# An attention and gated-FFN kernel: one group of heads of the second query block moved up to second place, more V tiles before the loop, later splitting of the exponentials, and finer background pieces

## The chip, the cores and the metric

The kernel runs on one core of a Trainium2 chip. The metric is the device time of one execution in microseconds; lower is better. The profile is of one execution.

## The reference

The input x has 2048 rows of 512 numbers. The layer normalises x, runs attention with 32 heads of 16 numbers, adds the result to x, normalises again, runs a gated feed-forward part with 1792 hidden columns, and adds that too.

```python
    h = x + _A_ref(_layernorm(x, axis=-1), A_wqkv, A_wo)
    h2 = h + _B_ref(_layernorm(h, axis=-1), B_w_gate, B_w_up, B_w_down)
...
        scores = jnp.einsum("bhqd,bhkd->bhqk", q, k) * (Dh ** -0.5)
        p = _softmax(scores, axis=-1)
        o = jnp.einsum("bhqk,bhkd->bhqd", p, v)
...
        h = _sigmoid(g) * u
        return jnp.einsum("bsf,fd->bsd", h, w_down)
```

## The kernel before, in words

**Units and groups.** The queries are cut into 4 blocks `qc` of 512, the heads into 8 groups `g` of 4, the keys into 16 tiles `kt` of 128. One unit is (qc, g, kt, j): 128 keys by 512 queries of head j of the group. The 2048 units stand in one list, block by block and group by group, 64 units to a group, and are taken three at a time as 683 tiles. A tile's scores go to three PSUM banks `pss` (two such buffers, L679); ScalarE takes their exponential into `pt` (five buffers, L828); TensorE multiplies `pt` with the V tile into the single accumulator `acc` (L747). When all 64 units of a group are in, `finish_group` transposes `acc` into `xs` on VectorE (L721), divides by the row sums, and after every second group turns the result into `OT`. Only then may the next group write `acc`.

**Splitting.** For some tiles the third unit's exponential is made on VectorE instead (`dexp_first`: one read of the scores, L761, and six more steps to `dr`, L781), and ScalarE takes two banks rather than three. `split` allows it only where the tile's last unit has `kt < NT - 4`, where no long VectorE work is pending, and where fewer than three such units are open.

**Background work.** Projections of K, Q and V, the output projection with the second normalisation (`wo_ln`), and the feed-forward part (`ffn`) are generators in one queue `bg`; its head advances when tokens and readiness allow, two matmuls at a time, through one PSUM bank `pm`. The order of all instructions is written by a planner in the kernel which keeps its own clocks `T["P"]`, `T["A"]` and `T["D"]` for TensorE, ScalarE and VectorE. `force(tag)` empties the queue down to a tag that the next scores or V products need. `prep_q` for block qc + 1 is inserted at position 1 of the queue, behind the item at its head, each time a pair of groups ends; `ffn(qc)` is one item. Q and K reach their place (`QT`, `KT`) by DMAs on SyncE's queue (`spread`, L172, then the row `sh`, L485); the shift row needs a maximum over K that also makes a trip by DMA (`k<-kr`, L451, then `kcol`, L454).

**When V products are issued.** Within the planner's time for one tile, `av` runs if six or more finished units are ready, or three or more after background work had its turn. A remainder of one or two at the end of a group waits until it is five tiles old (`NPT`) and is then forced.

**Before the loop.** A prologue normalises x, transposes it, makes K and Q of group 0 straight into place (`k0`, `proj0`) and the first six V tiles (`NV0`). The other V tiles, K and Q are background work, in the order V 6 to 9, K and Q of group 1, V 10 to 15, then K and Q of the other pairs. **After the loop** a tail does the last block's output projection and feed-forward part.

Of the kernel before, what the change touches and what calls it, by code (L numbers as in the profile page):

```python
# [10 lines left out]
BF16 = mybir.dt.bfloat16  # L11
# [3 lines left out]
ALU = mybir.AluOpType  # L15
# [13 lines left out]
def kernel(  # L29
# [47 lines left out]
    xnT = [const.tile([P, DC, QC], BF16, name=f"xnT{c}") for c in range(NQC)]  # L77
    KT = [const.tile([P, S], BF16, name=f"KT{g}") for g in range(NG)]
    QT = [const.tile([P, QC], BF16, name=f"QT{g}") for g in range(NG)]
    Vaug = const.tile([P, NT, H, VW], BF16)  # L80
    wq_sb = const.tile([P, DC, D], BF16)
    wo_sb = const.tile([P, NP, D], BF16)
    kcol = [const.tile([8, 1], FP32, name=f"kcol{p}") for p in range(NP)]
    o2buf = [const.tile([P, QC // 32, 32], BF16, name=f"o2_{i}") for i in range(2)]

    pre = ExitStack()
    prep = pre.enter_context(tc.tile_pool(name="prep", bufs=1))
# [91 lines left out]
    def v_out(ps, t, act):  # L179
        dst = Vaug[:, t, :, 0:DH]  # L180
        src = ps.rearrange("p (h d) -> p h d", d=DH)
        if act:
            nc.scalar.copy(out=dst, in_=src)
        else:
            nc.vector.tensor_copy(out=dst, in_=src)
# [6 lines left out]

    nc.scalar.activation(out=small.tile([P, 1], FP32, name="warm")[:], in_=eps_t[:], func=ACT.Sqrt)

    NV0 = 6
    mvs = [small.tile([P, TQ, nc.vector.BN_AGGR_DIM], FP32, name="mv") for c in range(NQC)]
    rstds = [small.tile([P, TQ], FP32, name="rstd") for c in range(NQC)]
    kmin = small.tile([P, NQC], FP32, name="kmin", bufs=1)
# [3 lines left out]
    def s0(c, *tiles):  # L202
        for i in tiles:
            ln_stats(xb[c][:, i, :], mvs[c][:, i, :])
# [43 lines left out]
    def kred0(c, pm):  # L248
        nc.vector.tensor_reduce(out=kmin[:, c:c + 1], in_=pm, axis=AX.X, op=ALU.min)

    def v0(t, act=True):
        ps = bank0()
        v_mm(ps, t)
        v_out(ps, t, act)

    s0(0, 0, 1, 2)
    act_stats(xb[0][:, 3, :], mvs[0][:, 3, :])
# [18 lines left out]
    s0(2, 1, 2, 3)  # L276
    rs0(2)
    pq, sqq = proj0(0, 1)
    nc.tensor.matmul(pq, lhsT=selq[:], rhs=sqq[:], start=False, stop=True, skip_group_check=True)
    pk1 = k0(1)  # L280
    s0(3, 0)
    a0(2)
    for i in range(TQ):
        t0(2, i)
    v0(0)
    s0(3, 1, 2, 3)
    rs0(3)
    pk2 = k0(2)
    v0(1)
    kred0(0, pk0)  # L290
    a0(3)
    for i in range(TQ):
        t0(3, i, i % 2 == 1)
    kred0(1, pk1)
    kred0(2, pk2)
    pk3 = k0(3, True)
    nc.scalar.activation(out=small.tile([P, 1], FP32, name="warm")[:], in_=eps_t[:], func=ACT.Exp)
    kred0(3, pk3)
    nc.vector.tensor_reduce(out=kfull[:], in_=kmin[:], axis=AX.X, op=ALU.min)
    nc.vector.tensor_scalar(out=QT[0][:], in0=pq, scalar1=kfull[:, 0:1], scalar2=None, op0=ALU.add)  # L300
    for t in range(2, NV0):
        v0(t, t % 2 == 0)
    for g in range(1, NG):
        ones_fill(g)
    ps0ctx.close()
# [7 lines left out]
    def pm_tile():  # L313
        return ps_m.tile([P, 512], FP32, name="pm")[:]
# [146 lines left out]
    def prep_q(qc, p, groups=(0, 1)):  # L461
# [131 lines left out]
        nc.scalar.activation(out=th[:], in_=ps, func=ACT.Tanh, scale=0.5)  # L593
        return th

    def ffn(qc):
        hT = fpool.tile([P, FC, QC], BF16, name="hT")
        th = {}
        for f in range(FC):
            yield pe(2, pm_new())  # L600
            ps = pm_tile()
            gate_mm(ps, wg, f, 0, 2)
            yield pe(2)
            gate_mm(ps, wg, f, 2, 4)
            ja = st["pm"] = act(530, lambda ps=ps, f=f: th.update({f: tanh_out(ps)}), st["mark"])
            yield pe(2, pm_new())
            ps = pm_tile()
            gate_mm(ps, wu, f, 0, 2)
            yield pe(2)
            gate_mm(ps, wu, f, 2, 4)  # L610
            st["pm"] = dve(700, lambda ps=ps, f=f: glu_out(hT, f, th[f], ps), st["mark"], ja)
        for i in range(TQ):
            ps = None
            for f in range(0, FC, 2):
                if (qc, i, f) == (NQC - 2, TQ - 1, 0):
                    yield pe(2, pm_new(), HOLD)
                else:
                    yield pe(2, pm_new() if f == 0 else None)
                if f == 0:
                    ps = pm_tile()  # L620
                down_mm(ps, hT, i, f, f + 2)
            st["pm"] = dve(700, lambda ps=ps, i=i: down_out(ps, qc, i), st["mark"])
        yield pe(0, st["pm"])

    HOLD = Mark(None)
    bg = deque()
    done = {("q", 0, 0)} | {("v", t) for t in range(NV0)}

    def queue(gen, tag, at=None):
        bg.insert(len(bg) if at is None else min(at, len(bg)), [gen, tag, None])  # L630
# [30 lines left out]
    def force(tag):  # L661
        while tag not in done:
            flush()
            try_bg(1e9, 1e12)

    units = [(qc, g, kt, j) for qc in range(NQC) for g in range(NG)
             for kt in range(NT) for j in range(4)]
    tiles = [units[i:i + GU] for i in range(0, len(units), GU)]

    readers = {}  # L670
# [1 line left out]

    def scores(n):
        for qc, g, kt, j in tiles[n]:
            if (qc, g) != (0, 0):
                force(("q", qc, g // 2) if (qc, g) != (0, 1) else ("q", 0, 0, 1))
        pss = ps_s.tile([P, GU, QC], FP32, name="pss")
        for ui, (qc, g, kt, j) in enumerate(tiles[n]):
            mm = nc.tensor.matmul(pss[:, ui, :],  # L679
                                  lhsT=KT[g][32 * j:32 * j + 32, kt * P:(kt + 1) * P],  # L680
                                  rhs=QT[g][32 * j:32 * j + 32, :],
                                  start=True, stop=True, tile_position=(32 * j, 0))
            for r in readers.get(n - 2, ()) if ui == 0 else ():
                tc.add_manual_dep(mm.ins, r.ins.name,
                                  DependencyInfo(DependencyClass.Sync, DependencyReason.DATA),
                                  reason="both readers of the bank's last scores")
        T["P"] = max(T["P"], ex_end.get(n - 2, 0.0) + LAT) + 380
        sc_end[n] = T["P"]
        return pss
# [9 lines left out]
    def finish_group(qc, g):  # L699
        xs = work.tile([P, QC // 32, 32], FP32, name="xs")  # L700
        p, a = divmod(g, 2)
        o2 = o2buf[p % 2]

        def norm():
            rec = small.tile([P, QC // 32, 1], FP32, name="rec")
            nc.vector.reciprocal(out=rec[:], in_=xs[:, :, DH:VW])
            nc.vector.tensor_tensor(out=o2[:, :, DH * a:DH * a + DH], in0=xs[:, :, 0:DH],
                                    in1=rec[:].to_broadcast([P, QC // 32, DH]), op=ALU.mult)

        def turn():  # L710
            ot = otp.tile([P, QC], BF16, name="ot")
            nc.vector.transpose(out=ot[:], in_=o2[:].rearrange("p b r -> p (b r)"))
            OT[qc, p] = ot
            if qc + 1 < NQC:
                queue(prep_q(qc + 1, p), ("q", qc + 1, p), 1)
                if p == NP - 2:
                    XR.extend(load_xr(qc, i) for i in range(2))
            if g == NG - 1 and qc < NQC - 1:
                queue(wo_ln(qc), ("wo", qc))
                queue(ffn(qc), ("f", qc))  # L720
        j = st["acc"] = dve(730, lambda: nc.vector.transpose(  # L721
            out=xs[:].rearrange("p b r -> p (b r)"), in_=acc[:]), Mark(T["P"]))
        j = dve(680, norm, j)
        if a:
            otj[qc, p] = dve(720, turn, j)

    def av_ready(loose):
        return [un for un in avq if un.u[0] * NG + un.u[1] == st["cur"] and un.end is not None
                and un.end + LAT <= T["P"] + loose]

    def av(limit, loose=60.0):
# [61 lines left out]
        nc.sync.dma_start(out=wd_[:], in_=B_w_down.rearrange("(f p) n -> p f n", p=P))  # L793
        return wg_, wu_, wd_

    for t in range(NV0, NV0 + 4):
        queue(prep_v(t), ("v", t))
    queue(prep_k(0, (1,)), ("k", 0))
    queue(prep_q(0, 0, (1,)), ("q", 0, 0, 1))
    for t in range(NV0 + 4, NT):  # L800
        queue(prep_v(t), ("v", t))
    for p in range(1, NP):
        queue(prep_k(p), ("k", p))
        queue(prep_q(0, p), ("q", 0, p))
# [7 lines left out]
    for n, tl in enumerate(tiles):  # L812
# [4 lines left out]
        while any(un.n <= n - NPT for un in avq):  # L817
            flush()
            if not av(8, 1e12):
                break  # L820
        start = max(T["A"], sc_end[n] + LAT)
        pend = sum(c[0] for c in chain)
        split = (len(tl) == GU and tl[-1][2] < NT - 4 and pend <= 900 and len(live_d) < 3
                 and max(T["D"], sc_end[n] + LAT) + pend <= start + 900
                 and sum(j.ns for j in dq if j.ready() is not None) <= 1500)
        wa = len(tl) - split
# [18 lines left out]
        while T["P"] < lim - 150:  # L845
            run_dve(min(T["P"], hor))
            ready = len(av_ready(60.0))
            if ready >= 6 and av(8):
                continue
            used = try_bg(tokens)  # L850
            if used:
                tokens -= used
                continue
            if ready >= 3 and av(8):
                continue
            T["P"] += 100
        run_dve(hor)
# [121 lines left out]
```

## Time and profile before

| what | value |
|---|---|
| median of 4 runs | 1079.19 us (1078.11 to 1080.51) |
| the profiled execution | 1078.11 us, its span 1076.3 us |
| busy TensorE, VectorE, ScalarE | 834.7, 750.6, 904.9 us |
| granted clock of TensorE, mean | 0.833 |

The span runs from the first to the last instruction. Busy time is the union of an engine's instructions, so instructions of one engine that overlap are counted once. An idle time is put down to the engine whose work ended it.

### The profile page before, as it was taken

The page shows a single profiled execution, that of the slowest core. Times are in us where ns is not written, and L with a number is a line of the kernel's source. Part 1 is how long each engine was busy: PE and PEld are TensorE (multiplying, and loading weights), DVE is VectorE, ACT ScalarE, POOL GpSimd, SP SyncE. Part 2 cuts the span into 40 slices and gives each one's busy share as a digit, 9 for nine tenths or more (in the row PEclk, how much of TensorE's full clock was granted, in tenths as well). Part 3 has the DMA queues.
Part 4 walks back from the last instruction along what each step waited for, and adds up shares of the span by engine and source line. Part 5 has one row for each costly group of instructions (what it writes and reads, how often), then busy time and mean ns, then how long its engine had stood idle before and what let it go on. Part 6 is the DMA issues. An engine that isn't in the chain of part 4 may idle for free.

```text
span 1076.3 us, 14506 instructions
## 1 busy us (share of the span) xinstructions
PE 834.7 (78%) x5137; PEld 231.4 (22%) x5213; DVE 750.6 (70%) x1854; ACT 904.9 (84%) x799; POOL 2.9 (0%) x7
## 2 busy tenths in 40 slices
PE   4858678677778788788687877877688787786868
PEld 2211122112112222222121222212122221221223
DVE  8936555777668887877877877766587777776441
ACT  6826699899889999999988999989799898998632
POOL 1000000000000000000000000000000000000000
PEclk9965788657568999989876998989877898896689
DMA  8010111600000000000000000000100000000000
GB/s 279 1 32 1 25 27 30 211 10 6 1 2 15 1 1 2 1 20 11 16 16 1 1 1 2 1 15 11 31 25 1 1 1 1 1 11 5 1 5 20
DMA packets 22048, 22.63 MB, mean 21 GB/s; under 512 B 4828, under 2 KB 20504, under 8 KB 21976
## 3 DMA queue, kind: packets, MB, share of 16 engines
q1 hardware_dynamic: 20344, 20.59, 6.6%
q10 hardware_dynamic: 1632, 1.11, 0.3%
q8 instruction: 41, 0.67, 0.3%
q14 instruction: 31, 0.25, 0.1%
HBM read 11.93 MB, written 2.10 MB: 13 GB/s over the span
## 4 chain that ended last, share of the span: by engine, by line
ACT 32%; PE 26%; DVE 20%; issue 16%; SPq 4%; DMA 2%; ACTq 0%; DVEq 0%
ACT pt L828 28%; PE pss L679 8%; PE acc L747 6%; DVE J L761 4%; DVE dr L781 3%; SPq L172 3%; PE pm L573 2%; PE pm L165 2%; ACT th L593 2%; DVE dq L779 2%; DVE db L777 2%; DVE da L770 1%; PE pm L176 1%; PE gu L573 1%; PE hp L944 1%
## 5 line engine op out<-in xcount | busy, mean ns | idle before, releaser
L828 ACT ACTIVATE pt<-pss 128x1536 bf16<-128x1536 f32 (+1 forms) x683 | 855.0, 1406 | 111.5 <-PE pss L679 74.4
L679 PE MATMUL pss<-QT,KT 32*128 32x512 bf16 x2048 | 309.6, 444 | 159.0 <-ACT pt L828 120.3
L747 PE MATMUL acc<-pt,Vaug 128*17 128x512 bf16 x1851 | 300.6, 454 | 8.2 <-DVE xs L721 7.3
L761 DVE TENSOR_SCALAR J<-pss 128x512 uint16<-128x512 f32 x197 | 134.8, 684 | 120.5 <-PE pss L679 119.7
L679 PEld LDWEIGHTS <-KT 32*128 32x128 bf16 x2048 | 89.8, 93 | 440.3 <-issue 333.7
L781 DVE SCALAR_TENSOR_TENSOR dr<-J,dq 128x512 uint16<-128x512 uint16 x197 | 135.4, 687 | 4.5
L747 PEld LDWEIGHTS <-Vaug 128*17 128x17 bf16 x2048 | 56.8, 89 | 194.8 <-issue 190.7
L747 PE MATMUL acc<-dr,Vaug 128*17 128x512 bf16 x197 | 84.4, 443 | 8.3 <-DVE xs L721 6.5
L779 DVE TENSOR_TENSOR dq<-dq,db 128x512 bf16<-128x512 bf16 x197 | 83.4, 423 | 6.1
L777 DVE TENSOR_TENSOR db<-da,db 128x512 bf16<-128x512 uint16 x197 | 81.8, 415 | 0.0
L770 DVE TENSOR_SCALAR da<-J 128x512 uint16<-128x512 uint16 x197 | 57.0, 289 | 4.4
L573 PE MATMUL pm<-xnT,wg 128*128 128x512 bf16 x178 | 55.4, 393 | 1.9 <-issue 0.8
L772 DVE TENSOR_SCALAR db<-J 128x512 uint16<-128x512 uint16 x197 | 55.9, 284 | 0.0
L774 DVE TENSOR_SCALAR dq<-da 128x512 bf16<-128x512 uint16 x197 | 55.8, 283 | 0.0
L577 DVE SCALAR_TENSOR_TENSOR hT<-th,pm 128x512 bf16<-128x512 f32 x42 | 28.7, 682 | 31.0 <-PE pm L573 27.0
L582 PE MATMUL pm<-wd,hT 128*128 128x512 bf16 x152 | 48.1, 398 | 2.6 <-issue 1.3
L573 PE MATMUL pm<-xnT,wu 128*128 128x512 bf16 x154 | 46.5, 388 | 2.0 <-issue 0.6
L593 ACT ACTIVATE th<-pm 128x512 f32<-128x512 f32 x49 | 34.7, 708 | 11.4 <-PE pm L573 11.3
L721 DVE STREAM_TRANSPOSE xs<-acc 128x512 f32<-128x512 f32 x32 | 22.7, 711 | 18.2 <-PE acc L747 18.2
L165 PE MATMUL pm<-xnT,wk_sb 128*128 128x512 bf16 x60 | 20.4, 431 | 5.4 <-DVE sh L482 2.7
L165 PE MATMUL pm<-xnT,wq_sb 128*128 128x512 bf16 x52 | 20.2, 466 | 4.9 <-issue 1.4
L573 PEld LDWEIGHTS <-wu 128*128 128x128 bf16 x224 | 17.1, 98 | 30.8 <-issue 20.8
(125 smaller groups left out, 399.9 us busy)
## 6 DMA issues: line engine op xcount, KB each, us to landing
KT<-ones SPq DMA_DIRECT2D x7, 512.0 KB
out_dram<-ob SPq DMA_DIRECT2D x16, 128.0 KB
QT<-qd SPq DMA_DIRECT2D x124, 16.0 KB
KT<-kd SPq DMA_DIRECT2D x28, 64.0 KB
wg<-in_B_w_gate_dram SPq DMA_DIRECT2D x1, 1792.0 KB
wu<-in_B_w_up_dram SPq DMA_DIRECT2D x1, 1792.0 KB
wd<-in_B_w_down_dram SPq DMA_DIRECT2D x1, 1792.0 KB
xr<-in_A_x_dram SPq DMA_DIRECT2D x12, 128.0 KB
```

Source lines behind the costliest of these rows:

```text
L165: nc.tensor.matmul(ps, lhsT=w_sb[:, d, p * P:(p + 1) * P], rhs=xnT[c][:, d, :], start=(d == 0), stop=(d == DC - 1))
L573: nc.tensor.matmul(ps, lhsT=w[:, d, f * P:(f + 1) * P], rhs=hnT[:, d, :], start=(d == 0), stop=(d == DC - 1))
L593: nc.scalar.activation(out=th[:], in_=ps, func=ACT.Tanh, scale=0.5)
L679: mm = nc.tensor.matmul(pss[:, ui, :], lhsT=KT[g][32 * j:32 * j + 32, kt * P:(kt + 1) * P], rhs=QT[g][32 * j:32 * j + 32, :], start=True, ...
L747: nc.tensor.matmul(acc[32 * j:32 * j + VW, :], lhsT=Vaug[:, kt, 4 * g + j, :], rhs=un.ap, start=(c == 0), stop=(c == NT - 1), tile_positio ...
L761: first = nc.vector.tensor_scalar(out=J[:], in0=src, scalar1=512 * SC * LOG2E, scalar2=512 * 127.0, op0=ALU.mult, op1=ALU.add)
L770: (215, lambda: V.tensor_scalar(out=a[:], in0=J[:], scalar1=511, scalar2=None, op0=ALU.bitwise_and)),
L772: (205, lambda: V.tensor_scalar(out=b[:], in0=J[:], scalar1=0xFE00, scalar2=None, op0=ALU.bitwise_or)),
L777: (440, lambda: V.tensor_tensor(out=b[:].bitcast(BF16), in0=a[:], in1=b[:].bitcast(I16), op=ALU.mult)),
L779: (450, lambda: V.tensor_tensor(out=q[:], in0=q[:], in1=b[:].bitcast(BF16), op=ALU.mult)),
L781: (620, lambda: V.scalar_tensor_tensor(out=r[:], in0=J[:], scalar=0.25, in1=q[:], op0=ALU.mult, op1=ALU.add)),
L828: ex = nc.scalar.activation(out=pt[:, 0:wa, :], in_=pss[:, 0:wa, :], func=ACT.Exp, scale=SC)
```

## The change

It has five parts. (1) The second group in the list becomes (1, 0): block 1, head group 0. Its keys are those of group 0; its queries come from a new `prep_q1` in the way of the prologue, into a new tile `QTb`, with no DMA. A third `o2buf` holds its half result. (2) The prologue makes ten V tiles, and V 0 to 5 stand between its other matmuls; V 10 to 15 are the first background work, then `prep_q1`, then K and Q of group 1. (3) `split` is allowed up to `kt < NT - 1`. (4) `ffn` becomes 14 items `ffn_up` and 4 items `ffn_down`, so that an insertion at position 1 falls between them. (5) `av` also runs when the ready units are all that is left of the group.

```diff
+    QTb = const.tile([P, QC], BF16)
-    o2buf = [const.tile([P, QC // 32, 32], BF16, name=f"o2_{i}") for i in range(2)]
+    o2buf = [const.tile([P, QC // 32, 32], BF16, name=f"o2_{i}") for i in range(3)]
...
-    NV0 = 6
+    NV0 = 10
...
     pq, sqq = proj0(0, 1)
+    pv0 = v0(0)
     nc.tensor.matmul(pq, lhsT=selq[:], rhs=sqq[:], start=False, stop=True, skip_group_check=True)
     pk1 = k0(1)
+    v_out(pv0, 0, True)
+    pv1 = v0(1)
     s0(3, 0)
     a0(2)
     for i in range(TQ):
         t0(2, i)
-    v0(0)
+    v_out(pv1, 1, True)
+    pv2 = v0(2)
...
+    def prep_q1():
+        yield pe(2, pm_new())
+        ps = pm_tile()
+        for d in range(DC):
+            if d == 2:
+                yield pe(2)
+            nc.tensor.matmul(ps, lhsT=w0p[:, 1, 4 * d:4 * d + 4, :], rhs=xnT[1][:, d, :],
+                             start=(d == 0), stop=(d == DC - 1))
...
+        st["pm"] = dve(660, lambda: nc.vector.tensor_scalar(
+            out=QTb[:], in0=ps, scalar1=kfull[:, 0:1], scalar2=None, op0=ALU.add), st["mark"])
+        yield pe(0, st["pm"])
...
-                queue(ffn(qc), ("f", qc))
+                for f in range(FC):
+                    queue(ffn_up(qc, f), ("f", qc))
+                for i in range(TQ):
+                    queue(ffn_down(qc, i), ("d", qc, i))
...
-    units = [(qc, g, kt, j) for qc in range(NQC) for g in range(NG)
-             for kt in range(NT) for j in range(4)]
+    gseq = [(0, 0), (1, 0)] + [(0, g) for g in range(1, NG)] + [(1, g) for g in range(1, NG)]
+    gseq += [(qc, g) for qc in range(2, NQC) for g in range(NG)]
+    units = [(qc, g, kt, j) for qc, g in gseq for kt in range(NT) for j in range(4)]
...
+    def av_last():
+        qc, g = gseq[st["cur"]]
+        return 4 * NT - sum(count.get((qc, g, j), 0) for j in range(4))
...
-    for t in range(NV0, NV0 + 4):
+    for t in range(NV0, NT):
         queue(prep_v(t), ("v", t))
+    queue(prep_q1(), ("q", 1, 0, 0))
     queue(prep_k(0, (1,)), ("k", 0))
     queue(prep_q(0, 0, (1,)), ("q", 0, 0, 1))
-    for t in range(NV0 + 4, NT):
-        queue(prep_v(t), ("v", t))
...
-        split = (len(tl) == GU and tl[-1][2] < NT - 4 and pend <= 900 and len(live_d) < 3
+        split = (len(tl) == GU and tl[-1][2] < NT - 1 and pend <= 900 and len(live_d) < 3
...
-            if ready >= 6 and av(8):
+            if (ready >= 6 or 0 < ready == av_last()) and av(8):
...
-            if ready >= 3 and av(8):
+            if (ready >= 3 or 0 < ready == av_last()) and av(8):
```

## Rows read from the trace of the kernel before

**Rows 1.** The page: the span, and each engine's busy time, share and instructions.

```profile
span 1076.3 us, 14506 instructions
PE 834.7 (78%) x5137; PEld 231.4 (22%) x5213; DVE 750.6 (70%) x1854; ACT 904.9 (84%) x799; POOL 2.9 (0%) x7
```

**Rows 2.** Groups by line and shape, ScalarE: busy us, mean ns; idle before, releasers.

```profile
L828 ACT ACTIVATE pt<-pss 128x1536 bf16<-128x1536 f32 x485 | 690.2, 1526 | 92.0 <-PE pss L679 55.8 <-PE acc L747 35.7
L828 ACT ACTIVATE pt<-pss 128x1024 bf16<-128x1024 f32 x198 | 218.3, 1111 | 19.4 <-PE pss L679 18.6
```

**Rows 3.** Who waited for whom, ScalarE: us in total, times, longest.

```profile
ACT pt L828 <- PE pss L679: 74.4, 52, 17.0
ACT pt L828 <- PE acc L747: 35.7, 21, 3.4
```

**Rows 4.** Stretches: length; busy PE, PEld, DVE, ACT, POOL (instructions); PEclk, DMA share, GB/s.

```profile
0.00:34.10 34.10, 18.61 (x118) 10.27 (x119) 27.04 (x82) 20.62 (x42) 2.90 (x7) 1.00 0.70 220
34.10:54.20 20.10, 16.76 (x108) 5.00 (x110) 19.18 (x46) 19.39 (x16) 0.00 (x0) 1.00 0.01 1
54.20:71.20 17.00, 7.73 (x28) 1.93 (x26) 7.03 (x16) 0.02 (x1) 0.00 (x0) 0.71 0.19 41
71.20:135.00 63.80, 47.60 (x234) 10.20 (x237) 34.24 (x79) 39.11 (x31) 0.00 (x0) 0.65 0.07 14
200.00:345.00 145.00, 112.97 (x686) 26.58 (x689) 105.04 (x264) 133.69 (x108) 0.00 (x0) 0.66 0.06 18
345.00:530.00 185.00, 150.93 (x1023) 42.47 (x1039) 144.92 (x361) 179.32 (x156) 0.00 (x0) 0.97 0.03 7
34.10:1013.70 979.60, 767.42 (x4806) 199.79 (x4875) 705.57 (x1737) 865.55 (x725) 0.00 (x0) 0.82 0.05 15
1013.70:1076.30 62.60, 48.68 (x215) 21.35 (x219) 17.96 (x36) 18.68 (x32) 0.00 (x0) 0.88 0.03 11
```

**Rows 5.** Timeline, the first two changes of group: start us, length us, instruction, idle before.

```profile
53.43 1.02 PE L165 MATMUL pm<-xnT,wk_sb 128*128 128x512 bf16 x3 [0.51 <-DVE kd L429]
...
63.49 0.14 DVE L454 TENSOR_REDUCE kcol<-k 8x1 f32<-8x4 f32 x1 [4.89 <-DMA k<-kr]
...
71.18 2.79 ACT L828 ACTIVATE pt<-pss 128x1536 bf16<-128x1536 f32 x2 [17.02 <-PE pss L679]
...
127.30 3.93 ACT L828 ACTIVATE pt<-pss 128x1024 bf16<-128x1024 f32 x3 [8.72 <-PE pss L679]
```

**Rows 6.** Timeline, where block 3 begins.

```profile
771.21 4.96 SPq L172 DMA_DIRECT2D QT<-qd  x8
772.38 0.74 DVE L482 TENSOR_SCALAR sh<-pm,kcol 8x512 bf16<-8x512 f32 x1 [2.85 <-DMA QT<-sh]
...
778.74 4.73 ACT L828 ACTIVATE pt<-pss 128x1024 bf16<-128x1024 f32 x4 [5.34 <-PE pss L679]
```

**Rows 7.** Timeline, the end of a group in the stretch without feed-forward work.

```profile
278.31 0.68 DVE L761 TENSOR_SCALAR J<-pss 128x512 uint16<-128x512 f32 x1
...
280.54 0.69 DVE L781 SCALAR_TENSOR_TENSOR dr<-J,dq 128x512 uint16<-128x512 uint16 x1
...
282.52 0.60 PE L747 MATMUL acc<-pt,Vaug 128*17 128x512 bf16 x1
283.15 0.72 DVE L721 STREAM_TRANSPOSE xs<-acc 128x512 f32<-128x512 f32 x1 [0.79 <-PE acc L747]
...
284.61 5.12 ACT L828 ACTIVATE pt<-pss 128x1536 bf16<-128x1536 f32 x4 [3.11 <-PE acc L747]
```

**Rows 8.** Timeline of the prologue.

```profile
7.37 0.37 SPq L104 DMA_DIRECT2D wv_sb<-in_A_wqkv_dram  x1
...
18.74 0.38 PE L279 MATMUL b<-sq,selq 128*128 128x512 bf16 x1 [0.69 <-ACT sq L233]
...
25.45 1.02 PE L176 MATMUL b<-wv_sb,xnT 128*128 128x512 bf16 x4
...
26.51 0.59 ACT L183 CAST Vaug<-b 128x512 bf16<-128x512 f32 x1 [0.75 <-PE b L176]
```

More of the change, by code (lines that the diff above doesn't have):

```diff
@@ L249, in kred0, with v0 @@
         nc.vector.tensor_reduce(out=kmin[:, c:c + 1], in_=pm, axis=AX.X, op=ALU.min)
-    def v0(t, act=True):
+    def v0(t):
         ps = bank0()
         v_mm(ps, t)
-        v_out(ps, t, act)
+        return ps
     s0(0, 0, 1, 2)
@@ L288 @@
     pk2 = k0(2)
-    v0(1)
+    v_out(pv2, 2, True)
+    pv3 = v0(3)
+    v_out(pv3, 3, True)
+    pv4 = v0(4)
     kred0(0, pk0)
@@ L295 @@
     kred0(2, pk2)
+    pv5 = v0(5)
     pk3 = k0(3, True)
     nc.scalar.activation(out=small.tile([P, 1], FP32, name="warm")[:], in_=eps_t[:], func=ACT.Exp)
+    v_out(pv4, 4, True)
+    v_out(pv5, 5, True)
     kred0(3, pk3)
@@ L300 @@
     nc.vector.tensor_scalar(out=QT[0][:], in0=pq, scalar1=kfull[:, 0:1], scalar2=None, op0=ALU.add)
-    for t in range(2, NV0):
-        v0(t, t % 2 == 0)
+    for t in range(6, NV0):
+        v_out(v0(t), t, t % 2 == 0)
     for g in range(1, NG):
@@ L487, in prep_q @@
         yield pe(0, st["pm"])
+    def prep_q1():
[6 more added lines that the diff above has]
+                             start=(d == 0), stop=(d == DC - 1))
+        qd = work.tile([P, QC], BF16, name="qd", bufs=2)
+        sq = work.tile([P, QC], BF16, name="sq", bufs=4)
+        j = dve(640, lambda: nc.vector.tensor_copy(out=qd[:], in_=ps), st["mark"])
+        j = dve(340, lambda: nc.vector.tensor_tensor(out=sq[:], in0=qd[:], in1=qd[:],
+                                                     op=ALU.mult), j)
+        yield pe(1, j)
+        nc.tensor.matmul(ps, lhsT=selq[:], rhs=sq[:], start=False, stop=True,
+                         skip_group_check=True)
+        st["pm"] = dve(660, lambda: nc.vector.tensor_scalar(
+            out=QTb[:], in0=ps, scalar1=kfull[:, 0:1], scalar2=None, op0=ALU.add), st["mark"])
+        yield pe(0, st["pm"])
     OT, otj = {}, {}
@@ L594, in tanh_out, with ffn_up, ffn_down @@
         return th
-    def ffn(qc):
-        hT = fpool.tile([P, FC, QC], BF16, name="hT")
-        th = {}
[L599 to L622, printed above, removed]
+    hts = {}
+    def ffn_up(qc, f):
+        yield pe(2, pm_new())
+        if f == 0:
+            hts[qc] = fpool.tile([P, FC, QC], BF16, name="hT")
+        hT = hts[qc]
+        th = {}
+        ps = pm_tile()
+        gate_mm(ps, wg, f, 0, 2)
+        yield pe(2)
+        gate_mm(ps, wg, f, 2, 4)
+        ja = st["pm"] = act(530, lambda: th.update({f: tanh_out(ps)}), st["mark"])
+        yield pe(2, pm_new())
+        ps2 = pm_tile()
+        gate_mm(ps2, wu, f, 0, 2)
+        yield pe(2)
+        gate_mm(ps2, wu, f, 2, 4)
+        st["pm"] = dve(700, lambda: glu_out(hT, f, th[f], ps2), st["mark"], ja)
+    def ffn_down(qc, i):
+        hT, ps = hts[qc], None
+        for f in range(0, FC, 2):
+            if f:
+                yield pe(2)
+            else:
+                yield pe(2, pm_new(), HOLD if (qc, i) == (NQC - 2, TQ - 1) else None)
+                ps = pm_tile()
+            down_mm(ps, hT, i, f, f + 2)
+        st["pm"] = dve(700, lambda: down_out(ps, qc, i), st["mark"])
         yield pe(0, st["pm"])
@@ L626 @@
     bg = deque()
-    done = {("q", 0, 0)} | {("v", t) for t in range(NV0)}
+    done = {("q", 0, 0, 0)} | {("v", t) for t in range(NV0)}
     def queue(gen, tag, at=None):
@@ L674, in scores @@
         for qc, g, kt, j in tiles[n]:
-            if (qc, g) != (0, 0):
-                force(("q", qc, g // 2) if (qc, g) != (0, 1) else ("q", 0, 0, 1))
+            force(("q", qc, 0, g) if qc < 2 and g < 2 else ("q", qc, g // 2))
         pss = ps_s.tile([P, GU, QC], FP32, name="pss")
@@ L680, in scores @@
                                   lhsT=KT[g][32 * j:32 * j + 32, kt * P:(kt + 1) * P],
-                                  rhs=QT[g][32 * j:32 * j + 32, :],
+                                  rhs=(QTb if (qc, g) == (1, 0) else QT[g])[32 * j:32 * j + 32, :],
                                   start=True, stop=True, tile_position=(32 * j, 0))
@@ L701, in finish_group @@
         p, a = divmod(g, 2)
-        o2 = o2buf[p % 2]
+        o2 = o2buf[2 if (qc, p) == (1, 0) else p % 2]
         def norm():
@@ L714, in turn @@
             if qc + 1 < NQC:
-                queue(prep_q(qc + 1, p), ("q", qc + 1, p), 1)
+                if (qc, p) == (0, 0):
+                    queue(prep_q(1, 0, (1,)), ("q", 1, 0, 1), 1)
+                else:
+                    queue(prep_q(qc + 1, p), ("q", qc + 1, p), 1)
                 if p == NP - 2:
@@ L725, in finish_group @@
             otj[qc, p] = dve(720, turn, j)
+    def av_last():
+        qc, g = gseq[st["cur"]]
+        return 4 * NT - sum(count.get((qc, g, j), 0) for j in range(4))
     def av_ready(loose):
-        return [un for un in avq if un.u[0] * NG + un.u[1] == st["cur"] and un.end is not None
+        return [un for un in avq if un.u[:2] == gseq[st["cur"]] and un.end is not None
                 and un.end + LAT <= T["P"] + loose]
```

## The prediction, made before the changed kernel was run

> **What bounds the kernel now.** I read the page first, then the stretches, then ScalarE's groups by shape, its waits, and the timeline at the longest of them. The page shows ScalarE as the busiest engine, 904.9 of 1076.3 us, with TensorE and VectorE behind it [rows 1]. The stretches show where that share is lost. The loop over the 683 tiles runs from 34.1 to 1013.7 us; in these 979.60 us ScalarE is busy 865.55, so it idles 114.05 us [rows 4]. Ahead of the loop lie 34.1 us, behind it 62.6 us, and 1078.11 - 1076.3 = 1.8 us lie outside the span. Per tile ScalarE's busy time is 865.55/683 = 1.267 us; it is 133.69/108 = 1.238 from 200 to 345 us and 179.32/142 = 1.263 from 345 to 530 (156 instructions, 14 of them tanh) [rows 4]. The reader is to see that this cost is steady, whatever TensorE's clock, so that the loop's time is tiles times 1.27 plus the idle time. Of the idle time the waits say what ended it: scores for 74.4 us, and V products, which free a `pt` buffer, for 35.7 [rows 3].
>
> The 114.05 us fall into four heaps. From 54.2 to 135 us ScalarE idles 17.00 + 63.80 - 0.02 - 39.11 = 41.7 us [rows 4]. In this early heap stand the wait of 17.02 us where group 1 needs K and Q that are still being projected and sent by DMA, and a second one of 8.72 us for the third group [rows 5]. The second heap is 5.34 us where block 3 begins and its Q is still on its way by DMA [rows 6]. The third is the 35.7 us on V products [rows 3]. The rest is 114.05 - 41.7 - 5.34 - 35.7 = 31.3 us in small pieces.
>
> How a piece of the third heap comes about can be seen at 278 to 285 us. TensorE has issued scores alone; at 282.52 a single V product is issued, the one that was left of a group of 64 = 21 x 3 + 1 units; `xs` follows at 283.15; and ScalarE, whose five `pt` buffers are full, has stood still for 3.11 us [rows 7]. The remainder was below three, so the planner held it until it was five tiles old.
>
> **The change part by part.**
>
> *The group (1, 0) in second place, V first.* It takes away what the 17.02 us wait is for: (1, 0) uses keys that are in place, and its Q needs no trip by DMA, where now VectorE stands for 4.89 us ahead of `kcol` [rows 5]. What it adds is five matmuls and three VectorE instructions of 0.74 us or less (as `sh` [rows 6]), and it leaves out the same for half a pair of Q. It must be ready at the end of group (0, 0). The first group ran 20.1 us with ScalarE busy 19.39 and TensorE 16.76 at full clock [rows 4], and it had some 28 background matmuls in it: the 16 of four V tiles, and of K's four chunks the third stands at its end, at 53.43 [rows 5]. The changed queue has there six V tiles (24 matmuls) and the five of Q, 29. So it is about in time. K and Q of group 1 are late next: about 25 matmuls, with the whole of (1, 0) for them, 21 tiles, which is again the same rate. The third and later pairs have one group's time more than now. I let 8 of the 41.7 us stay; the bounds are 2 (as in the first group, 0.71 us) and 20 (half).
>
> *Ten V tiles in the prologue.* Four more tiles are 16 matmuls, 1.02 us per tile at this clock, and four ScalarE copies of 0.59 us [rows 8]. In the prologue TensorE is busy 18.61 and ScalarE 20.62 of 34.1 us [rows 4], and TensorE waits 0.69 us for ScalarE's square at 18.74, just where the first added tile stands [rows 8]. So part is covered, and part comes ahead of matmuls that are on the chain: I take 2.3 us, bounded by 0.5 (nearly all in gaps) and 4.0 (no cover). V 0 now needs `wv_sb` at about 18 us; it was asked for at 7.37 [rows 8], and no row shows when it landed; a late landing belongs to the upper bound. What leaves the loop is four V tiles of background work, which lay beside a ScalarE that was busy 19.39 of 20.10 us: worth nothing by itself.
>
> *Splitting up to kt 14.* Tiles that may be split rise from 12 to 15 of 16, by a quarter. A split saves ScalarE 1526 - 1111 = 415 ns [rows 2] and costs VectorE 280.54 + 0.69 - 278.31 = 2.92 us [rows 7]. There are 198 short exponentials now, one of them the last tile, so 197 splits [rows 2]. VectorE is busy 705.57 us in the loop [rows 4]; 197 x 2.92 = 575 are these chains and 130 other work. In a loop of about 896 us it could hold none more if it stayed at the share of 345 to 530 us (144.92/185 = 78%: 699 - 130 = 569, 195 chains), and 50 more at that of the first group (19.18/20.10 = 95%). I take 27, in the middle, which loads it to (224 x 2.92 + 130)/896 = 88%. ScalarE saves 27 x 0.415 = 11.2 us, bounds 0 and 20.7. Of waits, the split units of kt 14 are the last to end in a group; three or four units of kt 14 and kt 15, two tiles of 1.27, still follow, about as long as the chain of 2.92, so `xs` is hardly later.
>
> *The remainder of a group.* It takes away the cause of the 35.7 us. I let 9 stay, for ends where VectorE or `xs` is late; bounds 3 and 20.
>
> *The feed-forward part in pieces.* Now the Q of the next block waits behind one long item, and each insertion at position 1 goes ahead of the one before. At 771 us the last of them sends eight DMAs, 4.96 us on SyncE's queue, and the scores wait for them [rows 6]. In pieces it goes ahead after the piece under way; its DMAs spread over groups and find the DMA engines nearly idle (share 0.03 to 0.06 from 200 to 530 us [rows 4]). SyncE's queue runs in order, and its other traffic there, the output rows, is issued in VectorE's order too. I let 0.5 of the 5.34 us stay. It issues no work more.
>
> *The small rest* of 31.3 us lies partly just behind the waits above (scores at the lower clock). I let 24 stay, bounds 14 and 31.3.
>
> **The clock, weighed.** Behind the wait of 17 us the granted clock is 0.65 in the mean from 71.2 to 135 us, between the two levels of 1.2 and 2.4 GHz, and TensorE needs 47.60/31 = 1.535 us per tile, more than ScalarE's 1.267 [rows 4]. From 200 to 345 us the clock is 0.66 as well, with TensorE busy for 112.97 of 145 us and no wait near 17 us; there it needs 1.046 us per tile, so ScalarE hides it [rows 4].
> The Trainium skill, "TensorE: Matmul & The Clock Gate", section "HAM oscillation — how this bites in real kernels", says that gaps between bursts of matmuls put the clock back to half and that a kernel pays for it after every gap. By that rule removing the gaps keeps the clock up throughout, and the sum would come out lower; the stretch from 200 to 345 us, where the clock is low at a high busy share, bears it out only in part. My sum goes by the rows.
>
> **The sum**, against the profiled execution: prologue 34.1 + 2.3 = 36.4; ScalarE in the loop 865.55 - 11.2 = 854.3; its idle time 8 + 0.5 + 9 + 24 = 41.5; tail 62.6; outside 1.8. Together 996.6 us, 7.6% under its 1078.11; the median of the runs shown, 1079.19, is 0.1% above that.
>
> **The rivals.**
>
> A. *The early wait moves.* K and Q of group 1, or `QTb`, are still late, a wait like the 8.72 us comes, and the clock falls behind it as it does now: from 71.2 to 135 us that costs 63.80 - 39.11 = 24.7 us [rows 4, 5]. The early heap is then 33.4 instead of 8: 996.6 + 25.4 = 1022. For it: the first group's background work is only just enough. Against it: V no longer stands behind K, so V products don't force it.
>
> B. *Group ends wait for VectorE.* The last split unit is late at half of the 31 ends between groups, 3.11 us each as at 284.61 [rows 7]: 15 x 3.11 = 47 instead of 9, that is 1034. For it: VectorE at 88%, and its work is queued in order. Against it: five `pt` buffers cover some 6 us.
>
> C. *Slower.* The same mechanism at every end: the late unit holds `acc`, and so all V products, until ScalarE has no `pt` buffer. It decides from (9 + 81.5)/31 = 2.9 us an end on, 81.5 being the whole gain; at the longest wait of now, 3.4 us [rows 3], the heap is 105 and the time 996.6 + 96 = 1093. Against it: a chain would have to end some 9 us after its scores, three times its length.
>
> D. *The clock stays up.* The loop idles as it does from 345 to 530 us, where the clock is 0.97: (185 - 179.32)/142 = 0.040 us per tile [rows 4], 27 us in all instead of 41.5: 982. For it: that stretch has background work all along, as more of the loop will. Against it: 200 to 345 us, as said. By the page of the Trainium skill named above it would go so.
>
> That splitting does not grow at all is no rival of its own: 11 us, within the range.
>
> **How the numbers follow.** Forecast 0.62, in 975 to 1015; A 0.14; B 0.09; C 0.03; D 0.12. The predicted time is the forecast's. Below it the bounds give 996.6 - 1.8 - 9.5 - 6 - 6 - 10 = 963; above it A and B reach to 1034, with a longer prologue and fewer splits to 1040. 963 to 1040 leaves out C and the tails of the others. Two executions of this kernel differ by about 0.2%, so less than that is no change. A, B, D and the forecast are all faster by far: 0.96; within 0.2%: 0.01; slower: 0.03.
>
> **What would show it.** In the changed profile ScalarE should have no wait above 6 us before 140 us; its waits for V products should total under 20 us; 128x1024 exponentials should number about 225; VectorE's share should rise towards 85%; the loop should begin at 35 to 38 us; no wait of scores for a Q DMA should stand where blocks 2 and 3 begin. It is wrong if splits crowd VectorE so that scores or group ends wait for it, if the early wait only moves, or if ScalarE's 1.27 us per tile rises.

## The result and the profile after

The changed kernel takes 969.20 us (median of 10 runs, 965.63 to 970.04) against 1076.74 us for the kernel before (16 runs): a ratio of 0.9002, 95% interval 0.8981 to 0.9023. It was forecast faster, at 996.6 us in a range of 963 to 1040. The profiled execution took 968.26 us.

The page of the changed kernel, as [rows 1]; its ScalarE groups by shape, as [rows 2]; and ScalarE's waits, as [rows 3]:

```profile
span 966.3 us, 14832 instructions
PE 799.9 (83%) x5141; PEld 233.6 (24%) x5218; DVE 833.9 (86%) x2105; ACT 886.9 (92%) x803; POOL 2.9 (0%) x7
```

```profile
L871 ACT ACTIVATE pt<-pss 128x1536 bf16<-128x1536 f32 x449 | 651.9, 1541 | 16.2 <-PE pss L713 12.1 <-PE acc L791 3.3
L871 ACT ACTIVATE pt<-pss 128x1024 bf16<-128x1024 f32 x234 | 262.5, 1126 | 3.3 <-PE pss L713 3.0
```

```profile
ACT pt L871 <- PE pss L713: 15.1, 29, 1.6
...
ACT pt L871 <- PE acc L791: 3.3, 2, 2.0
```

L871, L713, L791 and L805 are the old L828, L679, L747 and L761. The reader is to see three things: no wait of ScalarE for scores is longer than 1.6 us, where one was 17.0; the waits for V products fell from 35.7 to 3.3 us; and 234 exponentials are short, not 198. The stretches, with the columns of [rows 4]:

```profile
0.00:36.50 36.50, 22.27 (x130) 11.96 (x133) 27.07 (x82) 22.76 (x46) 2.90 (x7) 1.00 0.74 220
36.50:63.00 26.50, 23.49 (x156) 6.69 (x158) 25.57 (x62) 25.83 (x22) 0.00 (x0) 1.00 0.00 1
63.00:135.00 72.00, 58.46 (x386) 16.08 (x392) 50.29 (x121) 67.64 (x54) 0.00 (x0) 0.88 0.14 24
...
200.00:345.00 145.00, 121.17 (x741) 29.34 (x743) 131.60 (x339) 138.49 (x117) 0.00 (x0) 0.76 0.03 7
345.00:530.00 185.00, 159.41 (x1082) 46.26 (x1098) 174.48 (x445) 183.87 (x162) 0.00 (x0) 0.98 0.03 9
36.50:902.30 865.80, 727.31 (x4795) 199.70 (x4865) 788.90 (x1988) 845.43 (x725) 0.00 (x0) 0.92 0.06 16
902.30:966.30 64.00, 50.34 (x216) 21.96 (x220) 17.95 (x36) 18.70 (x33) 0.00 (x0) 0.87 0.03 11
```

The loop lasts 865.80 us instead of 979.60. ScalarE idles 865.80 - 845.43 = 20.4 us of it, where it idled 114.05, and is busy 20.1 us less. Most of what was won, 93.7 of 113.8 us, lies in the idle time. Up to 135 us ScalarE idles 26.50 + 72.00 - 25.83 - 67.64 = 5.0 us; before, 41.7 from 54.2 on [rows 4]. VectorE is busy 91% of the loop, up from 72%.

The new Q stands just in time. The timeline of the changed kernel where group (1, 0) begins:

```profile
58.71 0.75 DVE L516 TENSOR_SCALAR QTb<-pm,kfull 128x512 bf16<-128x512 f32 x1
...
62.09 0.39 PE L713 MATMUL pss<-QTb,KT 32*128 32x512 bf16 x2
```

It is written at 59.46 and first read at 62.09: 2.6 us to spare. And the end of a group, in the stretch that [rows 7] are from, now looks like this:

```profile
232.94 0.60 PE L791 MATMUL acc<-dr,Vaug 128*17 128x512 bf16 x1
...
233.34 0.63 PE L791 MATMUL acc<-pt,Vaug 128*17 128x512 bf16 x1
...
234.22 0.71 DVE L761 STREAM_TRANSPOSE xs<-acc 128x512 f32<-128x512 f32 x1
...
235.43 0.60 PE L791 MATMUL acc<-pt,Vaug 128*17 128x512 bf16 x1
```

The last two products of the group go out singly, 0.4 us apart, one of them with a VectorE unit (`dr`); `xs` follows at 234.22, and the next group's products start 1.2 us behind it. ScalarE runs through this end without a wait on V products. At two of the 31 ends it still waits for them, 1.98 and 1.35 us.

### The profile page after: what moved, and what is told of

Same layout as the page of the kernel before. It is cut to its first block, busy times and chain, and to the rows that moved or that the text cites. A ratio compares the mean times of both kernels' runs of the same rounds, so it can differ in the third digit from the quotient of the medians.

```text
span 966.3 us, 14832 instructions
## 1 busy us (share of the span) xinstructions
PE 799.9 (83%) x5141; PEld 233.6 (24%) x5218; DVE 833.9 (86%) x2105; ACT 886.9 (92%) x803; POOL 2.9 (0%) x7
## 4 chain that ended last, share of the span: by engine, by line
ACT 33%; DVE 28%; PE 22%; issue 16%; DMA 1%; SPq 0%; ACTq 0%; DVEq 0%
ACT pt L871 30%; PE pss L713 5%; DVE J L805 5%; PE acc L791 5%; DVE dr L825 5%; DVE dq L823 3%; DVE db L821 3%; PE pm L604 2%; DVE da L814 2%; PE pm L166 2%; DVE db L816 2%; DVE dq L818 2%; ACT th L624 2%; PE gu L604 1%; DVE hT L608 1%
## 5 line engine op out<-in xcount | busy, mean ns | idle before, releaser
L871 ACT ACTIVATE pt<-pss 128x1536 bf16<-128x1536 f32 (+1 forms) x683 | 835.3, 1399 | 19.5 <-PE pss L713 15.1
L713 PE MATMUL pss<-QT,KT 32*128 32x512 bf16 x1984 | 279.7, 412 | 112.6 <-ACT pt L871 84.3
L791 PE MATMUL acc<-pt,Vaug 128*17 128x512 bf16 x1815 | 301.3, 417 | 2.7 <-DVE xs L761 1.7
L713 PEld LDWEIGHTS <-KT 32*128 32x128 bf16 x2048 | 89.0, 92 | 388.7 <-issue 270.7
L805 DVE TENSOR_SCALAR J<-pss 128x512 uint16<-128x512 f32 x233 | 158.7, 681 | 11.8 <-PE pss L713 11.2
L825 DVE SCALAR_TENSOR_TENSOR dr<-J,dq 128x512 uint16<-128x512 uint16 x233 | 159.9, 686 | 4.9
L823 DVE TENSOR_TENSOR dq<-dq,db 128x512 bf16<-128x512 bf16 x233 | 98.6, 423 | 7.2
L791 PEld LDWEIGHTS <-Vaug 128*17 128x17 bf16 x2048 | 60.7, 88 | 166.3 <-issue 159.3
L791 PE MATMUL acc<-dr,Vaug 128*17 128x512 bf16 x233 | 95.8, 411 | 4.9 <-DVE dr L825 2.5
L821 DVE TENSOR_TENSOR db<-da,db 128x512 bf16<-128x512 uint16 x233 | 96.8, 415 | 0.0
L818 DVE TENSOR_SCALAR dq<-da 128x512 bf16<-128x512 uint16 x233 | 66.1, 284 | 0.0
L816 DVE TENSOR_SCALAR db<-J 128x512 uint16<-128x512 uint16 x233 | 66.0, 283 | 0.0
L604 PEld LDWEIGHTS <-wg 128*128 128x128 bf16 x224 | 16.9, 99 | 34.0 <-issue 26.1
L761 DVE STREAM_TRANSPOSE xs<-acc 128x512 f32<-128x512 f32 x32 | 22.7, 709 | 2.4 <-PE acc L791 2.2
```

Source lines behind the costliest of these rows:

```text
L604: nc.tensor.matmul(ps, lhsT=w[:, d, f * P:(f + 1) * P], rhs=hnT[:, d, :], start=(d == 0), stop=(d == DC - 1))
L713: mm = nc.tensor.matmul(pss[:, ui, :], lhsT=KT[g][32 * j:32 * j + 32, kt * P:(kt + 1) * P], rhs=(QTb if (qc, g) == (1, 0) else QT[g])[32 * ...
L791: nc.tensor.matmul(acc[32 * j:32 * j + VW, :], lhsT=Vaug[:, kt, 4 * g + j, :], rhs=un.ap, start=(c == 0), stop=(c == NT - 1), tile_positio ...
L805: first = nc.vector.tensor_scalar(out=J[:], in0=src, scalar1=512 * SC * LOG2E, scalar2=512 * 127.0, op0=ALU.mult, op1=ALU.add)
L816: (205, lambda: V.tensor_scalar(out=b[:], in0=J[:], scalar1=0xFE00, scalar2=None, op0=ALU.bitwise_or)),
L818: (205, lambda: V.tensor_scalar(out=q[:], in0=a[:], scalar1=EXP_C1 / (512 * 512 * 4), scalar2=EXP_C0 / (512 * 4), op0=ALU.mult, op1=ALU.add)),
```

## The experiments

Each was timed beside the kernel before on the same chip. First, parts of the change were taken back. The limit of kt 14 together with the held remainder, with the feed-forward part whole, or with the old order of groups was not tried; these were taken back from a version with the old limit.

**The split limit back to kt 11.**

```diff
-        split = (len(tl) == GU and tl[-1][2] < NT - 1 and pend <= 900 and len(live_d) < 3
+        split = (len(tl) == GU and tl[-1][2] < NT - 4 and pend <= 900 and len(live_d) < 3
```

> The changed kernel with the split limit put back to kt 11 (NT - 4), all else changed. Theory (each late split relieves ScalarE by 0.415 us, and VectorE has room): about 197 splits again instead of 233, so 36 x 0.415 = 15 us more, some 984 us; ScalarE's idle time stays near 20 us. Rival (late splits only crowd VectorE, or the room is taken from somewhere else): the time stays within 3 us of 969, or falls.

Measured: 985.68 us, ratio 0.9172 (0.9128 to 0.9216), as the theory has it. Short exponentials fell to 195; ScalarE is busy 861.97 us in the loop, 16.5 more for 39 short ones, 0.42 us each; its idle time is 23.0. Where VectorE's room came from is read from what VectorE waited for ahead of `J`, its first step of a split (us in total, times, longest): in the kernel before, in this one, in the changed one.

```profile
DVE J L761 <- PE pss L679: 119.7, 54, 7.4
```

```profile
DVE J L805 <- PE pss L713: 73.8, 25, 6.8
```

```profile
DVE J L805 <- PE pss L713: 11.2, 13, 2.5
```

These waits lie where a group ends: in the last quarter of a group (kt 12 to 15, from the fourth group on) VectorE idles 61% of the time in the kernel before, 64% in this one and 9% in the changed one. The new limit fills just this.

**The remainder held again**, with the old split limit.

```diff
-            if (ready >= 6 or 0 < ready == av_last()) and av(8):
+            if ready >= 6 and av(8):
...
-            if (ready >= 3 or 0 < ready == av_last()) and av(8):
+            if ready >= 3 and av(8):
```

> As the run with the split limit at kt 11, and without the rule that issues the last one or two V products of a group. Theory (the held remainder makes ScalarE wait for pt buffers, and the lower clock behind such waits makes more small waits): waits on V products 25 to 36 us again and 5 to 10 us more in small waits, 984 + 38 = about 1022 us. Rival 1 (only the waits themselves): 984 + 30 = 1014. Rival 2 (the denser background work of the new order leaves few remainders, so the rule does little): under 992.

Measured: 1029.37 us, 43.7 more than the run above in the same call. ScalarE's waits:

```profile
ACT pt L871 <- PE acc L791: 40.8, 22, 7.4
ACT pt L871 <- PE pss L713: 20.2, 35, 2.1
```

Waits on V products rose by 38.2 us (from 2.6) and those for scores by 7.7 (from 12.5). Of the waits for scores, ten, 7.3 us together, stand exactly four exponentials behind a wait on V products; with the rule none does. The theory holds, a little larger than expected; both rivals fall.

**The feed-forward part whole again**, with the old split limit.

```diff
-                for f in range(FC):
-                    queue(ffn_up(qc, f), ("f", qc))
-                for i in range(TQ):
-                    queue(ffn_down(qc, i), ("d", qc, i))
+                queue(ffn_all(qc), ("f", qc))
```

> As the run with the split limit at kt 11, and with the feed-forward part of a block as one item of the queue again. Theory (only the Q DMAs at the start of blocks 2 and 3 come late, as before): one or two waits of 1.5 to 6 us for Q there, 984 + 7 = about 991 us. Rival 1 (with one group less behind block 0, the whole feed-forward part must be flushed ahead of block 2's Q): one wait of 10 us or more there, above 996. Rival 2: no effect, within 2 us of 984.

Measured: 1004.66 us, 19.0 more than with the pieces. The size is rival 1's, the content not quite. Its timeline where block 2 begins:

```profile
476.98 0.69 DVE L618 SCALAR_TENSOR_TENSOR ob<-pm,h 128x512 bf16<-128x512 f32 x1 [3.17 <-PE pm L613]
...
477.72 1.02 PE L166 MATMUL pm<-xnT,wq_sb 128*128 128x512 bf16 x4 [0.46 <-DVE ob L618]
...
481.20 1.02 PE L166 MATMUL pm<-xnT,wq_sb 128*128 128x512 bf16 x4 [0.83 <-DVE sh L493]
...
487.75 1.86 PE L166 MATMUL pm<-xnT,wq_sb 128*128 128x512 bf16 x4 [3.71 <-DVE sh L493]
...
498.90 1.01 PE L719 MATMUL pss<-QT,KT 32*128 32x512 bf16 x5 [6.92 <-DMA QT<-sh]
...
499.61 2.37 ACT L874 ACTIVATE pt<-pss 128x1024 bf16<-128x1024 f32 x2 [20.97 <-PE pss L719]
```

The feed-forward part had just ended; what stood in the way are Q projections of three pairs one behind the other, the needed one last, each through the one bank `pm` and over the DMA queue. So with the new order of groups the pieces are worth 19 us, not the 5.34 us of [rows 6].

**The old order of groups**, with the old split limit.

```diff
-    gseq = [(0, 0), (1, 0)] + [(0, g) for g in range(1, NG)] + [(1, g) for g in range(1, NG)]
-    gseq += [(qc, g) for qc in range(2, NQC) for g in range(NG)]
+    gseq = [(qc, g) for qc in range(NQC) for g in range(NG)]
...
-    queue(prep_q1(), ("q", 1, 0, 0))
```

> As the run with the split limit at kt 11, and with the groups in the old order, block by block; ten V tiles in the prologue and V first in the queue stay. Theory (K and Q of group 1 need the time of group (1, 0)): a wait of 10 to 17 us where group 1 begins, a smaller one at the next pair, a low clock between 55 and 100 us; 984 + 25 = about 1009 us. Rival (V behind K was the trouble, and the V tiles made earlier cure it alone): no wait above 4 us there, under 992.

Measured: 994.06 us, 8.4 more than in the new order. The wait comes, in the lower half of what was expected:

```profile
75.20 2.37 ACT L866 ACTIVATE pt<-pss 128x1024 bf16<-128x1024 f32 x2 [12.63 <-PE pss L712]
```

What follows it is small: the next waits for scores above 1.2 us are of 1.26 and 1.48 us, and the granted clock from 55 to 100 us is 0.85 (0.89 with the moved group), not the low one expected. From 54.2 to 135 us ScalarE idles 16.1 us, where it idles 4.2 with the moved group and 41.7 in the kernel before. So 25.6 of the 41.7 us go without the moved group: by ten V tiles, by V ahead of K, and by the rule for the remainder, which alone takes 6.7 us there (below). V ahead of K was not tried by itself. The mechanism held, its size was a third of the expected.

**Six V tiles in the prologue**, from the changed kernel.

```diff
-    NV0 = 10
+    NV0 = 6
...
-    pv0 = v0(0)
...
-    v_out(pv0, 0, True)
-    pv1 = v0(1)
```

> The changed kernel with the old prologue (six V tiles, in their old places); V 6 to 15, then the Q of group (1, 0), are the first background work, 45 matmuls instead of 29 in group (0, 0). Theory (the first group holds some 28 to 30 of them, and the changed kernel has 2.6 us to spare): the loop begins 2 us earlier, and a wait of 8 to 14 us comes where group (1, 0) begins: about 969 - 2 + 11 = 978 us. Rival (the planner fits them in, as TensorE is idle an eighth of that group): no wait above 3 us, 967 us or less.

Measured: 973.99 us, ratio 0.9065 (0.9039 to 0.9090). The loop begins at 34.17 instead of 36.52, and where (1, 0) begins ScalarE waits:

```profile
66.71 7.31 ACT L861 ACTIVATE pt<-pss 128x1024 bf16<-128x1024 f32 x6 [6.11 <-PE pss L703]
```

The theory's mechanism, with a smaller wait than 8 to 14 us.

Then parts were put alone into the kernel before.

**The rule for the remainder alone** (the two lines above, the other way, with `av_last`).

> The kernel before with one part alone: V products also run when the ready units are all that is left of the group. Theory (the held remainder is the cause of the waits on pt buffers, and some small waits go with them): waits on V products fall from 35.7 to under 6 us, the small ones by 5 to 10, so 40 us less: about 1035 us, ratio 0.963. Rival (the waits move to another place, as VectorE's xs or the scores): ratio above 0.98.

Measured: 1010.90 us, ratio 0.9409 (0.9378 to 0.9439): 63 us of the change's 107, far more than expected. ScalarE's waits:

```profile
ACT pt L832 <- PE pss L679: 47.7, 35, 17.0
...
ACT pt L832 <- PE acc L751: 4.8, 3, 2.1
```

The waits on V products fell by 30.9 us, as expected, and those for scores by 26.7, which was not: the early wait of 17.0 stayed, but the 8.72 us of [rows 5] became 4.17 and the 5.34 us of [rows 6] disappeared. Where most of the rest went is shown in the next section, at the small rest.

**The limit at kt 13 alone** (`NT - 2`).

> The kernel before with the split limit moved from kt 11 to kt 13 alone (two thirds of the way of the change). Theory (VectorE has room, and a split saves ScalarE 0.415 us): 15 to 25 splits more, 6 to 10 us less, ratio 0.992. Rival (late split units are among the held remainder and make group ends wait longer): waits on V products above 40 us, ratio at or above 1.0.

Measured: 1055.67 us, ratio 0.9836 (0.9800 to 0.9872). Short exponentials: 225, 27 more; ScalarE is busy 11.7 us less, and idle 12.4 us less as well; waits on V products 31.8 us. Better than the theory; the rival falls. What shortens the idle time here is not known.

**The order, the prologue and V first, without the other parts** (the changed kernel with the first three diffs of this section together: the split limit, the held remainder, the whole feed-forward part).

> The changed kernel with only the new order of groups, the ten V tiles in the prologue and V first in the queue; split limit at kt 11, feed-forward part whole, remainder held. Theory: the early heap of 41.7 us falls to about 6, but the whole feed-forward part must be flushed ahead of block 2's Q, as in the run with it whole (a wait of 21 us): about 36 - 16 = 20 us less than before, ratio 0.98. Rival 1 (without the other parts the flush is small): ratio 0.965. Rival 2 (the flush and the held remainders together eat it all): ratio 1.0 or above.

Measured: 1069.83 us, ratio 0.9954 (0.9933 to 0.9975). No early wait is above 2.1 us up to 105 us, but one of 7.05 us on V products stands at 110.5, and from 54.2 to 135 us ScalarE idles 13.9 us, not some 6. Waits on V products are 46.4 us in all (35.7 before), and there is one of 20.94 us for block 2's Q, at 525 us:

```profile
ACT pt L874 <- PE pss L719: 55.4, 50, 20.9
...
ACT pt L874 <- PE acc L794: 46.4, 27, 7.0
```

Nearer to rival 2 than to the theory: what is won early is lost at group ends and at the Q pile.

Last, four variations of the changed kernel, to find what bounds it.

**Eight V tiles** (`NV0 = 8`).

> The changed kernel with eight V tiles in the prologue instead of ten; the two others become background work ahead of the Q of group (1, 0): 37 matmuls in group (0, 0). With six V tiles and 45 matmuls the wait was 6.1 us. Theory (some 2.6 us to spare, then each V tile costs 1.5 to 2.2 us): the loop begins 1.5 us earlier and a wait of 1 to 3 us comes; within 3 us of 969. Rival (the prologue's V tiles lie on its chain and the spare time covers two): 967 or less.

Measured: 969.22 us, ratio 0.9010 (0.8985 to 0.9034). A wait of 2.53 us at 63.8, a start at 35.73: the exchange that the theory has.

**Four open split units** (`len(live_d) < 4`, four `dr` buffers).

> The changed kernel with up to four split units open at a time and a fourth dr buffer, instead of three. Theory (VectorE's own time, 91 per cent busy in the loop, is what limits the splits): within 5 of 234 short exponentials, within 2 us of 969. Rival (the count of open units limits them): 10 or more splits more, 4 us or more less.

Measured: 967.35 us, ratio 0.8984 (0.8961 to 0.9006), 234 short exponentials: the count of open units is no limit.

**Looser limits of pending work** (1200 for 900 in `split`).

> The changed kernel with the planner's two limits for a split loosened from 900 to 1200 ns of pending VectorE work. Theory (ScalarE at 0.415 us per split is still the bound, VectorE has some 8 per cent left in the loop): 5 to 15 splits more, 2 to 6 us less, about 965 us. Rival (VectorE is now as much a bound as ScalarE, late split units make scores and group ends wait): more splits but the same time or a longer one, ScalarE's idle time above 25 us.

Measured: 970.48 us, ratio 0.9013 (0.8990 to 0.9036), 234 short exponentials again: neither the theory's splits nor the rival's, though ScalarE's idle time in the loop, 26.0 us, is what the rival has. What limits their number beyond VectorE's 91% is not settled.

**More background tokens** (1.6 per tile for 1.35).

> The changed kernel with 1.6 background matmuls per tile allowed instead of 1.35 from tile 72 on. Theory (background work is not on the path: ScalarE is 98 per cent busy): within 2 us of 969. Rival (the feed-forward part of a block finishes late, and finishing it earlier evens out the work): 4 us or more less; or more (matmuls in the way of scores): 3 us or more longer.

Measured: 974.25 us, ratio 0.9058 (0.9033 to 0.9083). Not the theory: it is 5 us longer, the size of the last rival, but not its cause. ScalarE idles 24.9 us; its waits for scores are 15.8 us (15.1 in the changed kernel), those on V products 6.1 (3.3), three of 2 us. No variation is clearly faster than the changed kernel.

## Why the prediction was right, and where its sum was off

The sum was 996.6 us, the profiled execution 968.26. This lies within 963 to 1040, near its lower end, but outside the 975 to 1015 that the forecast's own chance was for; rival D's 982 is nearer to it. The mechanisms came as described, but for the early wait; nearly every size came out on the same, better side. Term by term, forecast and measured:

| term | forecast | measured |
|---|---|---|
| prologue | 36.4 | 36.5 |
| ScalarE busy in the loop | 854.3 | 845.4 |
| ScalarE idle in the loop | 41.5 | 20.4 |
| tail and outside the span | 64.4 | 66.0 |

*Steady cost per tile times tiles, plus idle time.* Right: every run above is read that way, ScalarE's busy time in the loop lying between 845 and 866 us in all of them.

*The early heap.* 5.0 us stayed, 8 were forecast, and rival A did not come. But the wait of 17.02 us was misread. It does not stand where group 1 begins: by 54.2 us 16 exponentials had run [rows 4], and a group has 21 and a third, so it stands at kt 12 of the first group. From the trace of the kernel before:

```profile
52.53 0.38 PE L747 MATMUL acc<-pt,Vaug 128*17 128x512 bf16 x1
...
58.65 1.02 PE L165 MATMUL pm<-xnT,wq_sb 128*128 128x512 bf16 x4 [0.78 <-DVE kr L449]
...
66.34 1.86 PE L176 MATMUL pm<-wv_sb,xnT 128*128 128x512 bf16 x4 [0.83 <-DVE sh L482]
...
69.93 0.60 PE L747 MATMUL acc<-pt,Vaug 128*17 128x512 bf16 x2
...
70.46 1.03 PE L679 MATMUL pss<-QT,KT 32*128 32x512 bf16 x6
```

The V product after 52.53 needs V 10, which stood in the queue behind K and Q of group 1. `force` had all of these made first, and the next scores come behind that V product. So what removes this wait is V ahead of K; the text says as much against rival A, but gives the wait to the moved group. With V ahead of K and the old order of groups, K and Q of group 1 are late where group 1 does begin, 12.63 us, and it is this that the moved group removes. The 28 background matmuls, too, belong to 16 tiles of the first group; at that rate its 21 hold 37. "About in time" held for 29, with 2.6 us to spare; with 37 (eight V tiles) a wait of 2.53 us comes, with 45 (six) one of 6.11. The count was right, the working was not.

*The prologue.* 2.4 us against 2.3. V 0 ran at 18.43 us, and no wait there points to its weights.

*The splits.* 36 against 27, at 0.42 us as read; the nine more are 3.7 of the 8.9 us of busy time that the sum missed. The rest goes with the waits. ScalarE's exponentials overlap a little when one starts before the one ahead of it has ended. In the kernel before 546 of the 683 do, with the rule for the remainder alone 589, in the changed kernel 585; the union of all of them is 855.0, 851.5 and 835.3 us. With 0.415 us per split taken off, 4.7 us are left for 43 such starts more and 4.8 us for 39: an estimate of 0.11 to 0.12 us each. That fits; no run tests it alone.

*The remainder.* 3.3 us stayed of 9. Rivals B and C rested on late units of VectorE at group ends. With VectorE busy 91% of the loop that is what is left: at both ends that still wait, the last product of the group is one of a VectorE unit (317.95 and 720.24 us), and the other 29 don't wait.

*The feed-forward pieces.* No wait for Q remains, as forecast, but the price was read from the wrong case: 5.34 us belong to the old order; under the new one, at the old split limit, the pieces save 19 us, since the whole part ends only where block 2 begins. In the old order the rule for the remainder alone made the 5.34 us go. The text had not seen that the first part of the change needs the fourth.

*The step that was mis-sized: "the small rest".* 24 of 31.3 us were to stay; 20.4 - 5.0 - 3.3 = 12.1 did, below the bound of 14. The text saw that the small waits lie partly behind the large ones, but priced them as if they stayed when these went. In the kernel before, 15 of the 21 waits on V products are followed by one for scores exactly four exponentials later, 13.0 us together; with the rule for the remainder alone 0.5 us of this is left. One such pair, in the kernel before:

```profile
720.15 5.12 ACT L828 ACTIVATE pt<-pss 128x1536 bf16<-128x1536 f32 x4 [2.96 <-PE acc L747]
...
723.53 1.45 PE L747 MATMUL acc<-pt,Vaug 128*17 128x512 bf16 x8
...
724.92 1.03 PE L582 MATMUL pm<-wd,hT 128*128 128x512 bf16 x2
...
725.89 0.61 PE L679 MATMUL pss<-QT,KT 32*128 32x512 bf16 x3
...
726.61 2.79 ACT L828 ACTIVATE pt<-pss 128x1536 bf16<-128x1536 f32 x2 [1.33 <-PE pss L679]
```

Eight V products that had piled up and two background matmuls go ahead of the scores, and the granted clock is 0.50 from 717.5 to 726.6 us, against 0.99 in the 17 us ahead of it and 1.00 from 728 to 745; three scores take 0.61 us instead of 0.39. Which of the two makes the second wait was not separated. So a held remainder costs ScalarE twice. Of the 26.7 us of waits for scores that the rule alone takes away, these second waits are 12.5, the wait at block 3 is 5.34 and the shorter wait of the third group 4.55; why the last two shrink was not settled.

Two smaller slips: 1.29 of the 35.7 us on V products stand at 97 us, inside the early heap, so the small rest was 32.6; and the upper bound, with all of its terms, would be 1034 + 1.7 + 11.2 = 1047, not 1040.

*The clock.* From 200 to 345 us it is 0.76 with ScalarE busy 138.49 of 145 us; from 345 to 530 it is 0.98. So the row was the better guide: a low clock costs ScalarE little there. Rival D's idle time per tile (0.040 us) was reached and passed, 20.4/683 = 0.030, without its condition.
The Trainium skill's rule ("TensorE: Matmul & The Clock Gate", "HAM oscillation — how this bites in real kernels") agrees as far as the mean goes, 0.833 before and 0.917 with the long waits gone; the stretch at 0.76 has no such gap, as TensorE's longest idle time in it is 1.17 us.

## What to carry to other kernels

Where a planner holds back small remainders for efficiency, let the last of a group go as soon as it is ready: here two conditions gave 63 of the 107 us when put in alone, and 43.7 when taken out of a version that had the other parts but the split limit. The idle time that the trace put down to them, 35.7 us, was only half of the 63; look also for waits that follow such a wait at a fixed distance, here 13.0 us. See where in the group a wait stands before naming what it is for: the longest one stood five tiles ahead of the change of group that it was put down to. Price each part of a change within the change, not in the old kernel: the early parts alone (order, V tiles, V first) were worth 0.5%, and the new order made the feed-forward queue in pieces worth 3.6 times what the old trace showed. An engine that idles in a fixed part of each cycle, as VectorE in the last quarter of a group, is room that a condition and not the load keeps empty.

## What the runs showed of the hardware that was not expected

With TensorE at a mean granted clock of 0.66 (before) and 0.76 (after) from 200 to 345 us, ScalarE was busy 92 and 96% of that stretch; the lower clock alone did not make TensorE the bound. The granted clock can be at 0.50 for 9.1 us (717.5 to 726.6 in the kernel before) although no idle time of TensorE in that stretch is above 1.2 us; in the 5 us ahead of it TensorE had issued scores and some five background matmuls, and no V product. VectorE could be loaded from 78% of the loop (split limit at kt 11) to 91% while ScalarE's waits on V products stayed at 2.6 and 3.3 us.
